# Two buffers for the odd units' features in an output stage, and its five queues in another order

## The chip, the core and the metric

The kernel runs on one core of one Trainium2 chip. The metric is the device time of one execution in microseconds (us). Three executions of the kernel before took 2344.98 to 2349.98 us, with a median of 2349.86 us. The engines are named as the profile names them: PE (TensorE, matmul), PEld (its weight loads), DVE (VectorE), ACT (ScalarE), POOL (GpSimd) and SP (SyncE, which here issues every DMA transfer, in program order).

## The reference: what is computed

The reference adds to x a gated linear attention. With `xn = layernorm(x)`, x of 2048 rows and 1024 columns:

```python
q, k, v = split(xn @ wqkv)                      # 32 heads of 32
phi = lambda a: concat(softmax(a @ w_phi), softmax(-(a @ w_phi)))
num = phi(q) @ (phi(k)^T v)                     # per head, 64 features
den = phi(q) . sum(phi(k)) + 1e-6
s   = (num / den) @ wo                          # 1024 x 1024
g   = silu((sigmoid(xn @ w_gate) * (xn @ w_up)) @ w_down)
out = x + s * g
```

All arrays are float32. The change touches only the last stage, which makes `num / den`, multiplies it by `wo`, and forms `x + s * g`.

## The kernel before, in words

A float32 product is made of three matmuls on rounded halves (high times high, high times low, low times high; helper `mm3`, lines 151 to 153), so each operand is split into a high part (a cast on ACT) and a low part (a subtraction on DVE). The large products use seven products of half-size blocks in place of eight; their names are B11, T2, B21, T3, T1, T4, B22. Earlier stages make q, k, v, the features, the gate g (kept in the DRAM tensor `g_d`) and the split blocks of `wo` (kept in `wo_d`). The scaled features of q, already divided by the denominators and transposed, lie in the DRAM tensor `et_d`.

The output stage works on eight pairs of row tiles, 256 rows each (`NTP = 8`). Its loop runs seven times over a list of names called `PAIR`, and once over a list called `LAST` for the eighth pair. In one pass the seven products of pair t are multiplied while the numerators of pair t+1 are made:

- `gB110` to `gT43` are the products: seven blocks, four steps each, three matmuls per step, so 28 steps and 84 matmuls. `gB220-` to `gB223-` belong to the pair before (a `-` behind a name means the pair before, a `+` the next).
- `nm011`, `nm010` and so on are the numerators: `nm` with the half of the heads (0 or 1), the band (0 or 1) and the block. Each is four matmuls of 128x256 (line 1139), eight such steps a pair. `cp` and `ad` bring a result out of PSUM: a copy on ACT (line 1146) and an addition on DVE (line 1148).
- A unit is one half of the heads of one pair. Unit 2t is the even half of pair t, unit 2t+1 the odd half. Each unit has features of two kinds. Those of band 0 are loaded as one transfer of 512 KB into slot 47 and split by `hi` (ACT, line 1127) and `lo` (DVE, line 1129) into slots 44 and 45. Those of band 1 are loaded already split, as two transfers of 512 KB (function `e_load`, line 1121), into slots 20 and 21. The names are `e10` and `e00+` for the first kind, `e11` and `e01+` for the second.
- `s11`, `sA`, `sB`, `sC` are subtractions on POOL (line 1155) that make the left operands of the seven products, and `x...h`, `x...l` their splits (lines 1167 and 1169). T1 and T3 have slots 24 and 25 in even pairs and 39 and 40 in odd ones; B21 and B22 have 26 and 27, or 41 and 42.
- `c2`, `c3` copy a PSUM bank on ACT (line 1994); `v...` takes a result out; `m...` and `a...` multiply by g and add x on POOL (lines 2020 and 2021); `l...` loads a block of g and one of x (lines 1961 and 1962); `y...` stores a block of the output (line 2026).
- `w0` to `w3`, in the first pass alone, store the last four blocks of g from slots 0 to 3 and then load the four `wo` blocks of product B22 into these slots.

The order on each engine is that of the list: the context `in_order` ties every instruction of PE, DVE, ACT, POOL and SP to the one ahead of it on its engine. So an SP instruction that waits for a semaphore holds all later transfers, whatever they need.

Of the kernel before, what the change touches and what calls it, by code (L numbers as in the profile page):

```python
# [35 lines left out]
class Ring:  # L36
# [3 lines left out]
    def next(self):  # L40
        self.n += 1
        return self.items[(self.n - 1) % len(self.items)]
# [5 lines left out]
B11, T2, T3, B21, T1, T4, B22 = range(7)  # L48
# [3 lines left out]
def hedgehog_glu_kernel(  # L52
# [41 lines left out]
    slots, blocks, where = {}, {}, {}  # L94
# [27 lines left out]
    def whole(i):  # L122
        return slots[i].rearrange("p a n -> p (a n)")
# [3 lines left out]
    def halves(*ids):  # L127
        found = [(slots[i][:, a], i) for i in ids for a in range(2)]
        half_of.update((id(o), (o, i)) for o, i in found)
        return [o for o, _ in found]  # L130
# [975 lines left out]
          T1: [], T4: [], B22: list(range(4))}  # L1106
    res = Ring(halves(49, 52))
    nmr, amm = Ring(banks[:4]), Ring(banks[4:])
    e_next = [0, 0]
    oraw = [slots[50], slots[51]]  # L1110

    def wo_prep(i, k):
# [1 line left out]

    nbank = {}

    def e_load(q):
        tp_, hb = divmod(e_next[q], 2)
        if tp_ < NTP:
            for part, o in ((1, slots[21]), (2, slots[20])) if q else ((0, slots[47]),):  # L1120
                nc.sync.dma_start(o.bitcast(F32).rearrange("p b n -> p (b n)").rearrange("p (c x) -> p c x", c=8),
                                  et_d[tp_].rearrange("p u a (s h x) -> p s h (u a) x", s=3, h=2)[:, part, hb])
        e_next[q] += 1

    def phi_part(part):
        if part == "hi":
            nc.scalar.copy(whole(44), whole(47))
        else:
            nc.vector.tensor_sub(whole(45), whole(47), whole(44).bitcast(F32))

    def numerators(hb, q, b):

        ph = [whole((44, 20)[q] + a).rearrange("p (c k t) -> p c k t", k=4, t=32) for a in range(2)]
        kg = slots[KVB[hb]][:, q].rearrange("p (k m) -> p k m", m=P)
        nbank[hb, q, b] = ps = nmr.next()
        for j in range(2):
            k = 2 * j + b
            for a in range(2):
                nc.tensor.matmul(ps[:, j * 256:(j + 1) * 256], kg[:, k], ph[a][:, :, k], start=a == 0, stop=a == 1)  # L1139
# [15 lines left out]
        nc.gpsimd.tensor_sub(o, a, b)  # L1155

    def o_slot(tp_, i):
        a, b = ((24, 26), (39, 41))[tp_ % 2]
        return {B11: 46, T2: 22, T4: 23, T1: a, T3: a + 1, B21: b, B22: b + 1}[i]

    def o_part(tp_, name, part):
        i, n, b = {"B11": (B11, 1, oraw[0][:, 0]), "T2": (T2, 1, o_new[:, 1]), "T4": (T4, 1, o_new[:, 0]),
                   "T13": (T1, 2, oraw[0]), "B2": (B21, 2, oraw[1])}[name]
        o = run(o_slot(tp_, i), n)
        hi, lo = [o[:, :, a] if n > 1 else o[:, 0, a] for a in range(2)]
        if part == "h":
            nc.scalar.copy(hi, b)
        else:
            nc.vector.tensor_sub(lo, b, hi.bitcast(F32))

    def attend():

        def o_operand(i):
            for part in "hl":
                o_part(0, i, part)

        def numerator(hb, q):
            for b in range(2):
                numerators(hb, q, b)
                for part in ("cp", "ad"):  # L1180
                    numerators_out(part, hb, q, b)
            if (hb, q) == (0, 1):
                o_operand("B11")
                o_sum("s11")
            if (hb, q) == (1, 1):
                for f, a in ((o_sum, "sB"), (o_operand, "B2"), (o_operand, "T2"), (o_sum, "sA"), (o_sum, "sC"),
                             (o_operand, "T13"), (o_operand, "T4")):
                    f(a)

        out = []  # L1190
        for hb in range(2):
            out += [(int,)] * 4 + [(phi_part, "hi"), (phi_part, "lo"), (e_load, 0)]
            for q in range(2):
                out += [(numerator, hb, q)] + [(e_load, 1)] * q
        return out
# [4 lines left out]
    first = [halves(i) for i in (50, 51, 54, 38)]  # L1200
# [190 lines left out]
    @contextmanager  # L1391
    def in_order(*engines):

        traced = nc.cur_bb.bb.instructions
        last = traced[-1]
        yield
        begin = next(k for k in reversed(range(len(traced))) if traced[k] is last) + 1
        for i in traced[begin:]:
            if i.engine in engines:
                if i.engine in queued:  # L1400
                    tc.add_manual_dep(i, queued[i.engine].name,
                                      mybir.DependencyInfo(mybir.DependencyClass.NoSync, mybir.DependencyReason.DATA),
                                      reason="in_order")
                queued[i.engine] = i
# [481 lines left out]
    for n in range(TT):  # L1886
        t = (light if (n + 1) * QA // TT > n * QA // TT else heavy).popleft()
        for hb in range(2):
            q_late(2 + (2 * n + hb) * 24 // 5, t, hb)
    for n, (i, j, cs) in enumerate(dsteps):  # L1890
# [3 lines left out]
        for c in cs:  # L1894
            for u in range(4):
                p = 4 * c + u
# [8 lines left out]
        k, odd = divmod(n - (ND - 2 * NJ) - 9, 3)  # L1905
# [20 lines left out]
        if n == ND - NJ:  # L1926
            assert not plan and len(retired) == 2
            for b in (2, 5, 6):
                block(f"x{b}", 4 * b, 4, F32R)
            block("fb", 44, 3, F32R)  # L1930
            sig_r.items = [slots[53][:, 0]] + halves(38)
            step(1000)
            for q in range(2):
                e_load(q)
            side.extend([lambda fn=fn, a=a: fn(*a) for fn, *a in attend()])
# [21 lines left out]
    def gx_load(n):  # L1957
        if n < len(result) and result[n] not in gxs:
            t, cols = rows(*result[n])
            g, xt = gxs[result[n]] = halves(47) if n == len(result) - 1 else [gx[(2 * n + a) % 6] for a in range(2)]  # L1960
            nc.sync.dma_start(g, g_d[t, :, cols])
            nc.sync.dma_start(xt, x[t * P:(t + 1) * P, cols])

    for n in range(2):
# [4 lines left out]


    PAIR = """
        gB110 xT13h- xT13l- sC- gB111 hi0 lo0 e10 gB112 nm011 cp011 ad011 aT4- lT1- yT4- gB113 c2
        gB220- nm010 e11 cp010 gB221- xT4h- xT4l- ad010 gB222- gB223-
        gT20 vB22- mB22- w0 w1 gT21 nm001 aB22- lT4 yB22- cp001 ad001 gT22 gT23 c3
        gB210 nm000 w2 w3 cp000 ad000 gB211 hi1 lo1 e00+ gB212 vT2 xB11h xB11l s11 gB213
        gT30 vB21 aB21 lB22 yB21 gT31 nm111 cp111 ad111 gT32 nm110 e01+ cp110 ad110 gT33 vT3
        gT10 nm101 cp101 ad101 gT11 gT12 nm100 cp100 ad100 gT13
        gT40 vT1 sB xB2h xB2l gT41 sA xT2h xT2l gT42 mT1 aT1 lB21 yT1 gT43 vT4""".split()

    LAST = ("gB110 xT13h- xT13l- sC- aT4- lT1- yT4- gB111 gB112 gB113 c2 gB220- gB221- xT4h- xT4l- gB222- gB223- "  # L1980
            "gT20 vB22- mB22- gT21 aB22- lT4 yB22- gT22 gT23 c3 vT2 gB210 gB211 rest gB212 gB213 gT30 vB21 aB21 yB21 "
            "gT31 gT32 gT33 vT3 gT10 gT11 gT12 gT13 gT40 vT1 mT1 aT1 yT1 gT41 gT42 gT43 vT4 aT4 gB220 gB221 gB222 yT4 end").split()
    abank, ys = {}, {}

    def products(tp_, i, k):
        if k == 0 and i in (B11, T1):
            abank[tp_, i] = amm.next()
        o = [h.rearrange("p (k t) -> p k t", t=P) for h in pair(o_slot(tp_, i))]
        ps = abank[tp_, {B21: B11, T4: T3, B22: T1}.get(i, i)]
        mm3(ps, (o[0][:, k], o[1][:, k]), pair(WO[i][k]), i in (B11, T1) and k == 0, k == 3, skip_group_check=True)  # L1990
# [57 lines left out]
    def last_weights(k):  # L2048
# [7 lines left out]
    i_ = lambda n: operand_of[n]  # L2056
    pair_forms = (
        (r"nm(\d)(\d)(\d)", True, lambda p, h, q, b: numerators(int(h), int(q), int(b))),
        (r"(cp|ad)(\d)(\d)(\d)", True, lambda p, part, h, q, b: numerators_out(part, int(h), int(q), int(b))),
        (r"(s11|sA|sB|sC)", True, lambda p, n: o_sum(n)),  # L2060
# [12 lines left out]
    def take(tp_, names):  # L2073
        for name in names:
            off = {"-": -1, "+": 1}.get(name[-1], 0)
            if 0 <= tp_ + off < (NTP if names is LAST else NTP - 1):
                f, found = next((f, m) for form, _, f in pair_forms for m in [re.fullmatch(form, name.rstrip("+-"))] if m)
                f(tp_ + off, *found.groups())

    queued.clear()  # L2080
    with in_order(*[getattr(mybir.EngineType, e) for e in ("PE", "DVE", "Activation", "Pool", "SP")]):
        for tp_ in range(NTP - 1):
            take(tp_, PAIR)
        gx_load(len(result) - 1)
        take(NTP - 1, LAST)

# [29 lines left out]
```

## Time and profile before

| what | value |
|---|---|
| three runs | 2344.98, 2349.98, 2349.86 us |
| the profiled execution's own time | 2348.69 us |
| its span in the trace | 2346.8 us |
| PE busy over the span | 2308.6 us (98%) |
| POOL, ACT, DVE busy | 1213.7, 1229.0, 1660.2 us |
| mean granted TensorE clock | 0.991 |
| last waits of the stages before the output stage | until 2118.41 us |
| first numerator step of pass 0 | 2121.96 us |

Times in views of the trace count from the start of the span. In rows of the timeline the columns are start, duration, engine, line, operation, tiles and count; in brackets stand the idle time before it and what ended that. A row of the windows view gives a stretch, its length, the busy time of PE, PEld, DVE, ACT and POOL with instruction counts, the granted clock, the busy share of the DMA engines and GB/s. In rows on SP the duration is that of the issue, not of the transfer.

### The profile page before, as it was taken

How to read it: one execution, taken by the hardware profiler on the slowest of the kernel's cores; microseconds unless marked ns; L12 is line 12 of the kernel's file. 1: busy time of each engine (PE TensorE's matmuls, PEld its weight loads, DVE VectorE, ACT ScalarE, POOL GpSimd, SP SyncE). 2: the span in 40 equal slices, each digit the busy share in tenths (PEclk: the TensorE clock that was granted, in tenths of full speed). 3: DMA queues.
4: the chain of work that ended last, by engine and by line, in shares of the span. 5: the costliest groups of instructions: out<-in, count | busy, mean ns of one | idle time of the engine just before them, and what ended most of it. 6: DMA issues, size and time to landing. Idle time of an engine off the chain costs nothing.

```text
span 2346.8 us, 31513 instructions
## 1 busy us (share of the span) xinstructions
PE 2308.6 (98%) x10533; PEld 1920.5 (82%) x10533; DVE 1660.2 (71%) x1906; ACT 1229.0 (52%) x1907; POOL 1213.7 (52%) x934
## 2 busy tenths in 40 slices
PE   9999999999999999999999999999999999998888
PEld 8888888888888888888888888888888888886777
DVE  7625777886788775778874656556899888865665
ACT  7345577776555555555555455543454345454443
POOL 1324436772241055665653766755787557624555
PEclk9999999999999999999999999999999999998989
DMA  8789977988878777887886877769888778998774
GB/s 298 262 307 356 345 289 281 351 312 307 282 270 283 270 248 274 303 310 265 271 321 212 290 237 245 240 219 350 268 255 284 232 230 267 299 327 285 231 217 152
DMA packets 340530, 648.05 MB, mean 276 GB/s; under 512 B 36752, under 2 KB 86160, under 8 KB 335760
## 3 DMA queue, kind: packets, MB, share of 16 engines
q1 hardware_dynamic: 340368, 646.05, 80.3%
q8 instruction: 82, 1.34, 0.2%
q14 instruction: 80, 0.66, 0.1%
HBM read 386.73 MB, written 259.19 MB: 275 GB/s over the span
## 4 chain that ended last, share of the span: by engine, by line
PE 90%; DMA 4%; POOL 2%; DVE 2%; issue 1%; ACT 1%; SPq 0%; POOLq 0%; ACTq 0%; DVEq 0%
PE bank L151 29%; PE bank L153 29%; PE bank L152 29%; DMA x<-et_d 2%; PE bank L749 1%; POOL fc L1155 1%; PE bank L386 1%; PE bank L1139 1%; DMA fc<-et_d 0%; POOL fc L2020 0%; PE bank L254 0%; DMA fa<-wv 0%; POOL fb L2021 0%; DMA fa<-w_gu 0%; DVE fc L733 0%
## 5 line engine op out<-in xcount | busy, mean ns | idle before, releaser
L152 PE MATMUL bank<-x,w 128*128 128x512 f32 x2248 | 874.9, 389 | 0.0
L151 PE MATMUL bank<-x,w 128*128 128x512 f32 x2248 | 872.8, 390 | 1.4 <-ACT fc L1456 0.6
L153 PE MATMUL bank<-x,w 128*128 128x512 f32 x2248 | 873.1, 389 | 0.0
L143 DVE TENSOR_TENSOR w<-fa,w 128x512 fp32r<-128x512 f32 (+2 forms) x344 | 392.5, 1144 | 287.8 <-ACT w L142 276.5
L151 PEld LDWEIGHTS bank<-x,w 128*128 128x128 f32 x2248 | 422.0, 188 | 90.0 <-ACT fc L1456 1.9
L153 PEld LDWEIGHTS bank<-x,w 128*128 128x128 f32 x2248 | 421.9, 188 | 87.9
L152 PEld LDWEIGHTS bank<-x,w 128*128 128x128 f32 x2248 | 422.0, 188 | 87.2 <-DVE x L143 0.4
L142 ACT CAST w<-fa 128x512 fp32r<-128x512 f32 (+2 forms) x344 | 273.0, 796 | 328.6 <-PE bank L152 129.0
L151 PE MATMUL bank<-w,x 128*128 128x512 f32 x704 | 275.9, 392 | 0.0
L152 PE MATMUL bank<-w,x 128*128 128x512 f32 x704 | 274.6, 390 | 0.2 <-DVE w L1321 0.2
L153 PE MATMUL bank<-w,x 128*128 128x512 f32 x704 | 274.7, 390 | 0.0
L153 PEld LDWEIGHTS bank<-w,x 128*128 128x128 f32 x704 | 132.3, 188 | 28.2 <-DVE x L1311 0.7
L152 PEld LDWEIGHTS bank<-w,x 128*128 128x128 f32 x704 | 132.5, 188 | 27.0 <-DVE w L1321 0.6
L151 PEld LDWEIGHTS bank<-w,x 128*128 128x128 f32 x704 | 132.5, 188 | 26.3
L143 DVE TENSOR_TENSOR x<-fb,x 128x512 fp32r<-128x512 f32 (+1 forms) x121 | 126.6, 1049 | 24.6 <-ACT x L142 23.9
L143 DVE TENSOR_TENSOR w<-fb,w 128x512 fp32r<-128x512 f32 (+2 forms) x82 | 81.9, 1001 | 46.1 <-ACT w L142 43.6
L1155 POOL TENSOR_TENSOR fc<-fc 128x512 f32<-128x512 f32 x32 | 55.5, 1744 | 105.2 <-DVE fc L1148 68.2
L142 ACT CAST x<-fb 128x512 fp32r<-128x512 f32 (+1 forms) x121 | 86.3, 715 | 21.6 <-DMA fb<-xr_d 7.1
L1148 DVE TENSOR_TENSOR fc<-fc,bank 64x512 f32<-64x512 f32 x64 | 43.9, 686 | 65.3 <-ACT fc L1146 64.5
L143 DVE TENSOR_TENSOR p<-fc,p 128x512 fp32r<-128x512 f32 (+1 forms) x68 | 55.1, 820 | 45.8 <-ACT p L142 41.8
L1456 ACT COPY fc<-bank 128x512 f32<-128x512 f32 x116 | 66.5, 583 | 38.2 <-PE bank L153 16.2
L142 ACT CAST w<-fb 128x512 fp32r<-128x512 f32 (+2 forms) x82 | 50.2, 612 | 60.0 <-PE bank L152 38.8
(403 smaller groups left out, 3782.4 us busy)
## 6 DMA issues: line engine op xcount, KB each, us to landing
m_d<-fc SPq DMA_DIRECT2D x168, 256.0 KB, 4.6
fa<-h_d SPq DMA_DIRECT2D x82, 512.0 KB, 5.4
fa<-wf_d SPq DMA_DIRECT2D x32, 1024.0 KB, 7.2
x<-m_d SPq DMA_DIRECT2D x128, 256.0 KB, 4.7
fa<-w_gu SPq DMA_DIRECT2D x102, 256.0 KB, 5.2
h_d<-fc SPq DMA_DIRECT2D x102, 256.0 KB, 4.9
et_d<-x SPq DMA_DIRECT2D x64, 384.0 KB, 6.0
fc<-qkv_d SPq DMA_DIRECT2D x86, 256.0 KB, 5.2
```

The costliest lines, as they stand in the source:

```text
L142: nc.scalar.copy(o[0], src)
L143: i = nc.vector.tensor_sub(o[1], src, o[0].bitcast(F32))
L151: nc.tensor.matmul(o, a[0], b[0], start=first, stop=False, **kw)
L152: nc.tensor.matmul(o, a[0], b[1], start=False, stop=False, **kw)
L153: last_mm[:] = [nc.tensor.matmul(o, a[1], b[0], start=False, stop=last, **kw).ins]
L386: nc.tensor.matmul(ps[:, gs], r[:, gs], bd[:, 4 * f + g], start=g == 0, stop=g == 3, skip_group_check=True)
L749: nc.tensor.matmul(kvb[g // 2][:, g % 2 * 256:g % 2 * 256 + 256], v[:, g].rearrange("p a f -> p (a f)"), ph[:, g].rearrange("p a f -> p (a ...
L1139: nc.tensor.matmul(ps[:, j * 256:(j + 1) * 256], kg[:, k], ph[a][:, :, k], start=a == 0, stop=a == 1)
L1148: nc.vector.tensor_add(o, o, y)
L1155: nc.gpsimd.tensor_sub(o, a, b)
L1456: nc.scalar.copy(o, banks[b])
```

## The change

Band 1 of the odd units, from unit 3 on, goes to slots 39 and 40 in place of 20 and 21, so that even and odd units no longer share a buffer. For that T1 and T3 use slots 24 and 25 in all pairs. Unit 3 is loaded ahead of the loop. The names in `PAIR` and `LAST` stand in another order; `e11` becomes `e11+` and `hi0` becomes `hi0+`, so these are issued one pass earlier.

```diff
+    def feature_slots(unit):
+        return 39 if unit > 1 and unit % 2 else 20
...
-            for part, o in ((1, slots[21]), (2, slots[20])) if q else ((0, slots[47]),):
+            a = feature_slots(e_next[1])
+            for part, o in ((1, slots[a + 1]), (2, slots[a])) if q else ((0, slots[47]),):
...
-        ph = [whole((44, 20)[q] + a).rearrange("p (c k t) -> p c k t", k=4, t=32) for a in range(2)]
+        first = feature_slots(steps_of[1] // 2) if q else 44
+        steps_of[q] += 1
+        ph = [whole(first + a).rearrange("p (c k t) -> p c k t", k=4, t=32) for a in range(2)]
...
-        a, b = ((24, 26), (39, 41))[tp_ % 2]
-        return {B11: 46, T2: 22, T4: 23, T1: a, T3: a + 1, B21: b, B22: b + 1}[i]
+        b = (26, 41)[tp_ % 2]
+        return {B11: 46, T2: 22, T4: 23, T1: 24, T3: 25, B21: b, B22: b + 1}[i]
...
     PAIR = """
-        gB110 xT13h- xT13l- sC- gB111 hi0 lo0 e10 gB112 nm011 cp011 ad011 aT4- lT1- yT4- gB113 c2
-        gB220- nm010 e11 cp010 gB221- xT4h- xT4l- ad010 gB222- gB223-
-        gT20 vB22- mB22- w0 w1 gT21 nm001 aB22- lT4 yB22- cp001 ad001 gT22 gT23 c3
-        gB210 nm000 w2 w3 cp000 ad000 gB211 hi1 lo1 e00+ gB212 vT2 xB11h xB11l s11 gB213
-        gT30 vB21 aB21 lB22 yB21 gT31 nm111 cp111 ad111 gT32 nm110 e01+ cp110 ad110 gT33 vT3
-        gT10 nm101 cp101 ad101 gT11 gT12 nm100 cp100 ad100 gT13
-        gT40 vT1 sB xB2h xB2l gT41 sA xT2h xT2l gT42 mT1 aT1 lB21 yT1 gT43 vT4""".split()
+        gB110 xT13h- xT13l- gB111 lo0 e10 gB112 nm011 gB113 c2 cp011 ad011
+        gB220- nm010 cp010 ad010 aT4- lT1- yT4- gB221- gB222- gB223-
+        gT20 vB22- mB22- gT21 aB22- lT4 yB22- e01+ sC- gT22 nm001 gT23 c3 cp001 ad001
+        gB210 nm000 cp000 ad000 gB211 hi1 lo1 e00+ xT4h- xT4l- gB212 vT2 xB11h xB11l s11 gB213
+        gT30 vB21 aB21 lB22 yB21 w0 w1 gT31 nm111 cp111 ad111 gT32 nm110 e11+ cp110 ad110 gT33 vT3
+        gT10 w2 w3 gT11 nm101 cp101 ad101 gT12 nm100 cp100 ad100 gT13
+        gT40 vT1 sB xB2h xB2l gT41 sA xT2h xT2l hi0+ gT42 mT1 aT1 lB21 yT1 gT43 vT4""".split()
...
     with in_order(*[getattr(mybir.EngineType, e) for e in ("PE", "DVE", "Activation", "Pool", "SP")]):
+        phi_part("hi")
+        e_load(1)
         for tp_ in range(NTP - 1):
             take(tp_, PAIR)
```

In `LAST` the names `aT4- lT1- yT4-`, `sC-` and `xT4h- xT4l-` move later in the same way.

The first place is SP in a middle pass of the loop, from the store of T4 (`out<-fb`) on. `x_4` and `fa` are the two feature buffers of band 1 (slots 20 and 21, 39 and 40), `fc<-et_d` is the band 0 load, `g_d` and `x` are the loads of the gate and of x. Before:

```order
L2026 DMA out<-fb_0_99 128x512
L1121 DMA x_4_15714<-et_d 128x8x128 x2
L1961 DMA fc_101<-g_d 128x512
L1962 DMA fc_101<-x 128x512
L2026 DMA out<-fc_101 128x512
L1121 DMA fc_101<-et_d 128x8x128
L1961 DMA p_3_16019<-g_d 128x512
L1962 DMA p_3_16019<-x 128x512
L2026 DMA out<-fc_101 128x512
L1121 DMA x_4_15714<-et_d 128x8x128 x2
```

Now:

```order
L2032 DMA out<-fb_0_99 128x512
L1967 DMA fc_101<-g_d 128x512
L1968 DMA fc_101<-x 128x512
L2032 DMA out<-fc_101 128x512
L1125 DMA x_4_15714<-et_d 128x8x128 x2
L1125 DMA fc_101<-et_d 128x8x128
L1967 DMA p_3_16019<-g_d 128x512
L1968 DMA p_3_16019<-x 128x512
L2032 DMA out<-fc_101 128x512
L1125 DMA fa_16018<-et_d 128x8x128 x2
```

The first pair of band 1 rows of before is the odd unit of this pass (`e11`); now the first is the even unit of the next pass (`e01+`), and the second is the odd unit of the next pass (`e11+`) in its own buffer.

The second place is PE at the numerator steps of the odd half (`nm111` and `nm110`), around T3's products (`bank_108`):

```order
 L153 MATMUL bank_108<-x_6_15598,x_7_15715 128x512
-L1139 MATMUL bank_102<-x_4_15714,p_9711 128x256 x4
+L1145 MATMUL bank_102<-fa_16018,p_9711 128x256 x4
 L151 MATMUL bank_108<-x_6_15598,x_7_15715 128x512
 L152 MATMUL bank_108<-x_6_15598,x_7_15715 128x512
 L153 MATMUL bank_108<-x_6_15598,x_7_15715 128x512
-L1139 MATMUL bank_103<-x_4_15714,p_9711 128x256 x4
+L1145 MATMUL bank_103<-fa_16018,p_9711 128x256 x4
```

The steps stand where they stood, and read the new buffer.

The third place is SP in the first pass. `g_d<-x_5` are the last four stores of the gate, `x_6<-wo_d` the four loads of `wo` for B22. Before:

```order
L1121 DMA x_4_15714<-et_d 128x8x128 x2
L1961 DMA fc_101<-g_d 128x512
L1851 DMA g_d<-x_5_11982 128x512 x4
L1113 DMA x_6_16061<-wo_d 128x1024 x2
L1961 DMA p_3_16019<-g_d 128x512
L1962 DMA p_3_16019<-x 128x512
L1113 DMA x_6_16061<-wo_d 128x1024 x2
L1121 DMA fc_101<-et_d 128x8x128
L1961 DMA fc_101<-g_d 128x512
L1962 DMA fc_101<-x 128x512
L2026 DMA out<-fc_101 128x512
L1121 DMA x_4_15714<-et_d 128x8x128 x2
```

Now:

```order
L1125 DMA x_4_15714<-et_d 128x8x128 x2
L1125 DMA fc_101<-et_d 128x8x128
L1967 DMA fc_101<-g_d 128x512
L1968 DMA fc_101<-x 128x512
L2032 DMA out<-fc_101 128x512
L1857 DMA g_d<-x_5_11982 128x512 x4
L1113 DMA x_6_16114<-wo_d 128x1024 x2
L1125 DMA fa_16018<-et_d 128x8x128 x2
L1113 DMA x_6_16114<-wo_d 128x1024 x2
```

The stores and the four `wo` loads moved behind the store of B21 (`out<-fc`), and the band 1 load of the next pass (the last row of before, `e01+`) moved from behind them to ahead of them.

More of the change, by code (lines that the diff above doesn't have):

```diff
@@ L1108, in hedgehog_glu_kernel @@
     nmr, amm = Ring(banks[:4]), Ring(banks[4:])
-    e_next = [0, 0]
+    e_next, steps_of = [0, 0], [0, 0]
     oraw = [slots[50], slots[51]]
@@ L1971, in hedgehog_glu_kernel @@
     PAIR = """
-        gB110 xT13h- xT13l- sC- gB111 hi0 lo0 e10 gB112 nm011 cp011 ad011 aT4- lT1- yT4- gB113 c2
-        gB220- nm010 e11 cp010 gB221- xT4h- xT4l- ad010 gB222- gB223-
-        gT20 vB22- mB22- w0 w1 gT21 nm001 aB22- lT4 yB22- cp001 ad001 gT22 gT23 c3
-        gB210 nm000 w2 w3 cp000 ad000 gB211 hi1 lo1 e00+ gB212 vT2 xB11h xB11l s11 gB213
-        gT30 vB21 aB21 lB22 yB21 gT31 nm111 cp111 ad111 gT32 nm110 e01+ cp110 ad110 gT33 vT3
-        gT10 nm101 cp101 ad101 gT11 gT12 nm100 cp100 ad100 gT13
-        gT40 vT1 sB xB2h xB2l gT41 sA xT2h xT2l gT42 mT1 aT1 lB21 yT1 gT43 vT4""".split()
-    LAST = ("gB110 xT13h- xT13l- sC- aT4- lT1- yT4- gB111 gB112 gB113 c2 gB220- gB221- xT4h- xT4l- gB222- gB223- "
-            "gT20 vB22- mB22- gT21 aB22- lT4 yB22- gT22 gT23 c3 vT2 gB210 gB211 rest gB212 gB213 gT30 vB21 aB21 yB21 "
+        gB110 xT13h- xT13l- gB111 lo0 e10 gB112 nm011 gB113 c2 cp011 ad011
[5 more added lines that the diff above has]
+        gT40 vT1 sB xB2h xB2l gT41 sA xT2h xT2l hi0+ gT42 mT1 aT1 lB21 yT1 gT43 vT4""".split()
+    LAST = ("gB110 xT13h- xT13l- gB111 gB112 gB113 c2 aT4- lT1- yT4- gB220- gB221- gB222- gB223- "
+            "gT20 vB22- mB22- gT21 aB22- lT4 yB22- sC- gT22 gT23 c3 vT2 gB210 xT4h- xT4l- gB211 rest gB212 gB213 gT30 vB21 aB21 yB21 "
             "gT31 gT32 gT33 vT3 gT10 gT11 gT12 gT13 gT40 vT1 mT1 aT1 yT1 gT41 gT42 gT43 vT4 aT4 gB220 gB221 gB222 yT4 end").split()
```

## The prediction

> **What bounds the kernel now.** I read the page first (the span and its slices), then the waits of PE, then the windows of the output stage, and last the timeline around one wait.
>
> ```profile
> span 2346.8 us, 31513 instructions
> PE   9999999999999999999999999999999999998888
> PEclk9999999999999999999999999999999999998989
> ```
>
> PE is full for 36 slices and falls to eight tenths in the last four, which are the output stage; the granted clock dips in the same slices. Only there is time to be had. The waits of PE from 2085 us to the end name the cause:
>
> ```profile
> PE bank L1139 <- DMA x<-et_d: 26.6, 6, 7.9
> ```
>
> The six waits, each with its idle time in brackets, and the stretches between them:
>
> ```profile
> 2151.02 1.19 PE L1139 MATMUL bank<-x,p 128*128 128x256 f32 x4 [7.88 <-DMA x<-et_d]
> 2192.86 0.72 PE L1139 MATMUL bank<-x,p 128*128 128x256 f32 x4 [2.84 <-DMA x<-et_d]
> 2221.89 0.98 PE L1139 MATMUL bank<-x,p 128*128 128x256 f32 x3 [4.12 <-DMA x<-et_d]
> 2250.86 0.77 PE L1139 MATMUL bank<-x,p 128*128 128x256 f32 x2 [4.30 <-DMA x<-et_d]
> 2280.14 0.77 PE L1139 MATMUL bank<-x,p 128*128 128x256 f32 x2 [3.81 <-DMA x<-et_d]
> 2309.93 0.81 PE L1139 MATMUL bank<-x,p 128*128 128x256 f32 x3 [3.67 <-DMA x<-et_d]
> ```
>
> ```profile
> 2123.33:2142.98 19.65, 19.46 (x98) 16.16 (x96) 11.39 (x14) 9.92 (x17) 7.17 (x6) 1.00 0.80 266
> 2142.98:2192.86 49.88, 38.48 (x179) 31.89 (x178) 28.04 (x32) 20.48 (x31) 28.03 (x18) 0.90 0.79 242
> 2192.86:2221.89 29.03, 24.91 (x116) 20.74 (x117) 17.80 (x19) 12.75 (x19) 15.95 (x10) 0.93 0.72 222
> 2221.89:2250.86 28.97, 24.67 (x117) 20.65 (x117) 17.80 (x19) 12.75 (x19) 15.96 (x10) 0.91 0.72 218
> 2250.86:2280.14 29.28, 25.47 (x116) 21.29 (x117) 17.80 (x19) 12.74 (x19) 15.97 (x10) 0.91 0.69 211
> 2280.14:2309.93 29.79, 26.12 (x116) 21.79 (x117) 17.80 (x19) 12.74 (x19) 15.96 (x10) 0.90 0.69 212
> 2309.93:2346.80 36.87, 32.40 (x145) 27.07 (x145) 14.75 (x19) 8.50 (x13) 18.86 (x14) 0.92 0.40 137
> ```
>
> The first wait stands at nm011 of the second pass (the even unit), the other five at nm111 of the passes after it (the odd unit). Why the odd unit is late shows in the queue ahead of its two loads:
>
> ```profile
> 2208.92 2.27 POOL L1155 TENSOR_TENSOR fc<-fc 128x512 f32<-128x512 f32 x1
> 2211.15 1.29 POOL L2021 TENSOR_TENSOR fb<-fb,fc 128x512 f32<-128x512 f32 x1
> 2212.85 0.42 SPq L2026 DMA_DIRECT2D out<-fb  x1
> 2213.37 1.78 SPq L1121 DMA_DIRECT2D x<-et_d  x2
> ```
>
> POOL does sC, then aT4; the store of T4 waits for that until 2212.44, and the feature loads stand behind the store in SP's order. They go out at 2213.37, and PE gets them at 2221.89, 8.5 us later. They could not go out long before either: both units share slots 20 and 21, so nm010 must have read the even unit first.
>
> **The price of one wait** is more than the idle time, since PE runs slower behind it. Behind the 1.89 us wait that opens the stage:
>
> ```profile
> 2118.41 0.50 PE L151 MATMUL bank<-x,fb 128*128 128x512 f32 x1 [1.89 <-DVE x L1878]
> 2120.26 0.63 PE L153 MATMUL bank<-x,fb 128*128 128x512 f32 x1
> 2120.68 0.63 PE L151 MATMUL bank<-x,fb 128*128 128x512 f32 x1
> 2122.65 0.39 PE L151 MATMUL bank<-x,fb 128*128 128x512 f32 x1
> 2122.88 0.39 PE L152 MATMUL bank<-x,fb 128*128 128x512 f32 x1
> ```
>
> Matmuls start 0.42 us apart at 2120 and 0.23 apart at 2122.65, so a product step of three costs 0.69 us at full clock. The undisturbed stretch 2123.33 to 2142.98 (clock 1.00) holds 23 such steps, 15.9 us, and seven numerator steps, which leaves 0.54 us for each of these. A whole pair has five steps and one numerator step more: 19.65 + 3.45 + 0.54 = 23.6 us. The four middle pairs take 29.03, 28.97, 29.28 and 29.79; take off each one's wait, and PE is still busy for 24.91, 24.67, 25.47 and 26.12, that is 1.1 to 2.5 us over 23.6: the slow clock.
>
> The Trainium skill ("TensorE: Matmul & The Clock Gate", part 1 on the HAM clock gate) has the clock fall to half after an idle window of about 3.4 us, and come back after a like time of work. The halving and the length of the slow spell agree with these rows; that a wait of 1.89 us is enough does not, and the measurement decides. By that rule, small waits that remain would cost only themselves.
>
> **What the change takes away.** Edit by edit.
>
> - *Own buffer for odd units, loads a pass ahead.* `e11+` goes out behind nm110 and the store of B21 of the pass before, and is wanted at the next nm111, nearly a whole pair later (some 17 us). `e01+` goes out behind the store of B22, some 15 us ahead of its old place. Both landed within 9.7 us at worst:
>
> ```profile
> DMA to landing us min/median/max: 4.3/6.4/9.7
> ```
>
>   So I take all six waits as gone. The four middle pairs give 117.07 - 4 x 23.6 = 22.7 us. The wait at 2192.86 gives its 2.84. Behind 2309.93 there are 42 product steps and four numerator steps, 29.0 + 2.2 = 31.2 us, against 32.40 busy: 1.2. Together 26.7 us for the five odd waits. The first wait gives 7.88 and its slow spell: the stretch to 2192.86 holds 43 product and 12 numerator steps, 29.7 + 6.5 = 36.2 us, against 38.48 busy: 2.3; together 10.2. The sum is 36.9 us.
>
> - *T1 and T3 in one buffer.* The split `xT13` of a pass stands behind gB110 and the last read of the old operands, gT13, four product steps (2.8 us) ahead of it. Nothing waits: cost 0, at most some 0.5 us if ACT ran that far ahead.
>
> - *sC and xT4 later.* sC now comes behind aB22 on POOL, about 6.6 us behind gB223; the T4 operand is wanted at gT40, some 13 us behind gB223. POOL is busy for 16 us of a pair, so it keeps up at 23.6. Cost 0; without that cover, xT4 is late by what POOL is late.
>
> - *w0 to w3 later, in the first pass only.* Here is a new wait.
>
> ```profile
> 2133.66 1.30 POOL L2021 TENSOR_TENSOR fc<-fc 128x512 f32<-128x512 f32 x1
> 2126.68 2.70 SPq L1851 DMA_DIRECT2D g_d<-x  x4
> 2133.89 0.80 SPq L1113 DMA_DIRECT2D x<-wo_d  x2
> 2140.58 3.30 SPq L1121 DMA_DIRECT2D x<-et_d  x2
> x<-wo_d SPq DMA_DIRECT2D x16, 512.0 KB, 7.1
> ```
>
>   Before, the four stores of g go out from 2126.68 and the first `wo` load 7.2 us later, since it overwrites what they read. Now they stand behind aB21, which ends at 2134.96, and its store: from about 2135.4. The first `wo` load then goes out at about 2142.6, the fourth, behind the two `e11+` loads, at about 2145.6, and lands 7.1 us later at 2152.7. Products reach gB223 of the second pass, free of the old wait, at 2142.98 + 0.54 + 0.69 (nm011, gB113) + 3 x 0.69 + 0.54 = 2146.8. So PE waits 5.9 us in gB220 to gB223, and the slow spell adds 2.3: 8.2 us. Bounds: 0 if stores and loads land much faster on a quieter queue, 10.2 if all lands as late as 2155. I take 8.2, the value of the median landing. What is queued behind these loads on SP (lB21, yT1, `e10`) is not wanted before vB21 and hi1, which this wait delays as well.
>
> - *hi0 a pass earlier, unit 3 ahead of the loop.* 1 MB more ahead of eight `wo` loads that are wanted 20 us later, and one cast of 1.05 us at a place where ACT is half idle (12.7 of 29 us busy). Cost 0.
>
> The sum: 2348.69 - 36.9 + 8.2 = 2320.0. The median of the runs shown is 1.2 us above the profiled execution, so 2321 us, 1.2% less.
>
> **What is the limit next.** The band 0 features still have one slot, and their load `e10` stands in SP behind the store of T1. This closes a loop:
>
> ```profile
> 2199.37 0.64 PE L1139 MATMUL bank<-fb,p 128*128 128x256 f32 x4
> 2200.04 0.58 ACT L1146 COPY fc<-bank 64x512 f32<-64x512 f32 x1 [1.26 <-PE bank L1139]
> 2201.49 3.53 POOL L1155 TENSOR_TENSOR fc<-fc 128x512 f32<-128x512 f32 x2 [8.85 <-DVE fc L1148]
> 2206.80 2.16 POOL L2021 TENSOR_TENSOR fc<-fc 128x512 f32<-128x512 f32 x1
> 2210.07 0.52 SPq L1121 DMA_DIRECT2D fc<-et_d  x1
> 2216.09 1.05 ACT L1127 CAST fb<-fc 128x1024 fp32r<-128x1024 f32 x1 [1.15 <-DMA fc<-et_d]
> 2217.18 1.23 DVE L1129 TENSOR_TENSOR fb<-fc,fb 128x1024 fp32r<-128x1024 f32 x1 [1.45 <-ACT fb L1127]
> ```
>
> From nm100 over cp, ad, sB, sA, mT1, aT1, yT1, `e10`, its landing (6.0 us from issue to hi1) and lo1 it takes 2218.41 - 2199.37 = 19.0 us; nm101 and one step follow, 1.2 us, and nm100 stands again: 20.3 us. That is under 23.6, with 3.3 us to spare. Before, the waits of 4 us hid it.
>
> **Rivals.**
>
> *The band 0 loop or the DMA engines take part of it back.* A pair keeps the DMA engines busy for 0.71 of 29 us, 20.6 us; in 23.6 us that is 0.87, so landings may lengthen. The spare 3.3 us are gone when `e10` takes 9.3 us, near the longest landing seen. At 10 us each pass waits 0.7 us at nm101 and pays some 1.7 us of slow clock: six times 2.4 is 14, and the time 2335. For it: hi1 already waited 1.15 us for this load. Against: its landing sits in a gap of the queue, behind transfers of only 0.75 MB. With the skill's rule the clock would stay up, and the time be 2321 + 6 x 0.7 = 2325.
>
> *The `wo` loads are not late.* Then 8.2 us more is gained: 2313. For it: stores of 256 KB from a quiet queue. Against: the 7.2 us above.
>
> *No change.* The wait moves to another operand by as much as it was (`xT4` behind a late POOL, say, since sC, s11 and sB now follow each other closely): pairs of 29 us, 2347. POOL's 16 us speak against it.
>
> *Slower.* The same loop, with landings above 13.3 us: then a pair is 20.3 - 6.0 + 13.3 + 1.7 = 29.3 us, as now. At 15 us it is 31, five pairs lose 8.5 us, less the 2 won in the second pass: 2356. It needs a queue that stays full while loads run a pass ahead; a share of 0.87 speaks against it.
>
> **Chances.** Forecast 0.62 (its own range 2315 to 2329), loop in part 0.20, no late `wo` loads 0.08, no change 0.05, slower 0.05. About 0.2%, or 4.7 us, is what a measurement can tell here. Faster is 0.62 + 0.20 + 0.08 = 0.90, same 0.05, slower 0.05. The range runs from all waits gone with no new one (2312, and 1 us of spread) to somewhat beyond the second case: 2311 to 2339.
>
> **What would show it.** Right: no wait of L1139 for `x<-et_d` or `fa<-et_d`; pairs of 23.6 to 24.5 us with the clock at 1.00; one wait of 4 to 8 us on a DMA of `wo_d` near 2145; DMA share near 0.87. Wrong: waits at nm101 for lo1 (L1129 in before), a clock below 0.95 in the middle pairs, PE waits on xT4's split, or SP held behind `e01+` so that g or x come late for vB21.

## The result and the profile after

The changed kernel takes 2312.78 us (median, 2311.92 to 2313.67); the kernel before, beside it, 2347.42 us (2343.85 to 2349.98). The ratio is 0.9854, with a 95% interval of 0.9836 to 0.9871: 1.5% faster. The forecast was 2321 us, 1.2% less. The time lies 2.2 us below the forecast's own range (2315 to 2329) and near the low end of the wide one (2311 to 2339).

The page of the changed kernel, its span and PE's slices:

```profile
span 2311.7 us, 31526 instructions
PE   9999999999999999999999999999999999999899
PEclk9999999999999999999999999999999999999999
```

The fall over the last four slices is gone, but for one slice, and so is the dip of the clock. All that PE waits for from 2085 us to the end:

```profile
PE bank L151 <- DMA x<-wo_d: 5.9, 2, 5.7
PE bank L151 <- DVE x L1884: 1.7, 1, 1.7
PE bank L151 <- DVE x L1175: 1.3, 1, 1.3
PE bank L151 <- ACT bank L2000: 0.2, 1, 0.2
```

No wait for `et_d` is left. The windows of the changed kernel, one pass of the loop each, from nm111 to nm111, and the rest (columns as before: length, busy PE, PEld, DVE, ACT, POOL, granted clock, DMA share, GB/s):

```profile
2160.78:2183.92 23.14, 23.14 (x118) 19.59 (x116) 16.18 (x19) 11.67 (x18) 16.00 (x10) 1.00 0.74 227
2183.92:2207.05 23.13, 23.13 (x117) 19.58 (x116) 17.28 (x20) 12.74 (x20) 16.02 (x10) 1.00 0.91 270
2207.05:2230.18 23.13, 23.13 (x117) 19.58 (x116) 17.12 (x20) 12.61 (x19) 16.00 (x10) 1.00 0.92 275
2230.18:2253.32 23.14, 23.14 (x118) 19.58 (x116) 16.91 (x19) 12.19 (x19) 16.01 (x10) 1.00 0.89 270
2253.32:2276.45 23.13, 23.13 (x117) 19.58 (x116) 17.52 (x20) 13.25 (x21) 16.02 (x10) 1.00 0.90 274
2276.45:2311.70 35.25, 30.78 (x146) 25.66 (x144) 17.12 (x23) 9.86 (x16) 21.93 (x15) 1.00 0.45 150
```

Each pass takes 23.13 us and PE is busy for all of it; before it took 29.0 to 29.8. From the second of these passes on the DMA engines work at 0.89 to 0.92 of their time.

The wait that the change adds stands in the second pass (timeline of PE, and SP's four `wo` loads):

```profile
2136.57 0.79 SPq L1113 DMA_DIRECT2D x<-wo_d  x2
2137.46 1.24 SPq L1125 DMA_DIRECT2D fa<-et_d  x2
2138.74 5.16 SPq L1113 DMA_DIRECT2D x<-wo_d  x2
2140.04 0.47 PE L151 MATMUL bank<-x,x 128*128 128x512 f32 x1 [1.25 <-DVE x L1175]
2141.64 0.50 PE L151 MATMUL bank<-x,x 128*128 128x512 f32 x1 [0.19 <-DMA x<-wo_d]
2148.32 0.79 PE L151 MATMUL bank<-x,x 128*128 128x512 f32 x1 [5.73 <-DMA x<-wo_d]
2149.34 0.63 PE L153 MATMUL bank<-x,x 128*128 128x512 f32 x1
2154.78 0.39 PE L153 MATMUL bank<-x,x 128*128 128x512 f32 x1
```

PE waits 5.73 us and runs at half clock until 2154.5: the 15 matmuls from 2148.32 to 2155.01, where nm001 starts, take 6.7 us in place of 3.4 (15 times 0.23), so 3.3 us more.

Where the 35.1 us between the two spans come from: the first product of the loop (gB110) starts at 2118.41 before and at 2114.43 after, and from there it takes 228.4 and 197.3 us. So 31.1 us are the output stage. The other 4.0 were there well before: SP issues the same load of `w_down` at 2069.92 before and at 2065.94 after, and the first load that the change adds, that of unit 3, goes out only at 2103.13. The experiment on the kernel before, below, bears on them.

### The profile page after: what moved, and what is told of

Read it like the earlier page. It is cut to its first block, busy times and chain, and to the rows that moved or that the text cites. A ratio compares the mean times of both kernels' runs of the same rounds, so it can differ in the third digit from the quotient of the medians.

```text
span 2311.7 us, 31526 instructions
## 1 busy us (share of the span) xinstructions
PE 2294.9 (99%) x10533; PEld 1911.0 (83%) x10533; DVE 1664.3 (72%) x1906; ACT 1231.0 (53%) x1907; POOL 1219.2 (53%) x934
## 5 line engine op out<-in xcount | busy, mean ns | idle before, releaser
L143 DVE TENSOR_TENSOR w<-fa,w 128x512 fp32r<-128x512 f32 (+2 forms) x344 | 397.5, 1159 | 294.3 <-ACT w L142 273.5
L151 PE MATMUL bank<-w,x 128*128 128x512 f32 x720 | 282.0, 392 | 0.0
L153 PE MATMUL bank<-w,x 128*128 128x512 f32 x720 | 280.9, 390 | 0.0
L152 PE MATMUL bank<-w,x 128*128 128x512 f32 x720 | 280.6, 390 | 0.0
L153 PEld LDWEIGHTS bank<-w,x 128*128 128x128 f32 x720 | 135.2, 188 | 29.2 <-DVE x L1317 1.0
L152 PEld LDWEIGHTS bank<-w,x 128*128 128x128 f32 x720 | 135.3, 188 | 26.9 <-DVE w L1327 0.3
L151 PEld LDWEIGHTS bank<-w,x 128*128 128x128 f32 x720 | 135.2, 188 | 26.6
L1161 POOL TENSOR_TENSOR fc<-fc 128x512 f32<-128x512 f32 x32 | 49.8, 1566 | 78.0 <-DVE fc L1154 33.3
```

The costliest lines, as they stand in the source:

```text
L143: i = nc.vector.tensor_sub(o[1], src, o[0].bitcast(F32))
L151: nc.tensor.matmul(o, a[0], b[0], start=first, stop=False, **kw)
L152: nc.tensor.matmul(o, a[0], b[1], start=False, stop=False, **kw)
L153: last_mm[:] = [nc.tensor.matmul(o, a[1], b[0], start=False, stop=last, **kw).ins]
```

## The experiments

**The `wo` loads of the first pass earlier.** Of the changed kernel, only the place of the last stores of g (`ws`) and of the loads for B22 is another:

```diff
-        ... lT4 yB22- e01+ sC- gT22 ...
+        ... lT4 yB22- e01+ ws sC- gT22 ...
-        ... hi1 lo1 e00+ xT4h- ...
+        ... hi1 lo1 e00+ w0 w1 w2 w3 xT4h- ...
-        gT30 vB21 aB21 lB22 yB21 w0 w1 gT31 ...
-        gT10 w2 w3 gT11 ...
+        gT30 vB21 aB21 lB22 yB21 gT31 ...
+        gT10 gT11 ...
```

> The changed kernel, but in the first pass the four stores of g go out behind the first e01+ loads, and the four wo loads of B22 behind e00+, about 6 us earlier than in the changed kernel (where the first goes out at 2136.57 and the wait for the third or fourth ends at 2148.32). Theory: the 5.9 us of PE waits on wo_d in the second pass are the price of moving w0 to w3 behind the store of B21, and nothing else waits there; without them PE also keeps its full clock behind (12 matmuls at 0.43 us apart now, 2.7 us lost). Expected: no PE wait on wo_d, 2304 to 2306 us. Rival: the DMA engines are simply full in the first pass, so the loads land as late whenever they go out, or e01+ and lB22 come late instead: 2311 to 2315, with a wait of like size on another load.

Measured: 2304.3 us (2303.07 to 2305.73), ratio to the kernel before 0.9826 (0.981 to 0.9843). SP and all of PE's waits from 2085 us on:

```profile
2133.58 1.74 SPq L1113 DMA_DIRECT2D x<-wo_d  x4
```

```profile
PE bank L151 <- DVE x L1884: 1.8, 1, 1.8
PE bank L151 <- ACT bank L2000: 0.2, 1, 0.2
```

Counted from gB110 (2115.64 here, 2114.43 in the changed kernel) the first of these loads goes out after 17.9 us in place of 22.1, the last by 19.7 in place of 29.5, and no wait on `wo_d` or anything behind it is left. The theory holds: late `wo` loads were the price of the change. The medians put it at 8.5 and 9.0 us (against the two measurements of the changed kernel, 2312.78 and, below, 2313.25), the ratios to the kernel before at 6.6 and 8.2; the prediction had 8.2. This version is the fastest of all that ran.

It also shows what the 1.25 us wait ahead of gB220 in the changed kernel is. The profile names a split on DVE (`DVE x L1175`); here gB220 (second row) starts without a wait while that split still runs:

```profile
2139.47 1.67 DVE L1175 TENSOR_TENSOR x<-fc,x 128x1024 fp32r<-128x1024 f32 x1
2139.84 0.40 PE L151 MATMUL bank<-x,x 128*128 128x512 f32 x1
```

So gB220 does not need the split, and its wait belongs to the `wo` loads as well.

**One buffer, new order.** The changed kernel with slots 20 and 21 for all units:

```diff
-        return 39 if unit > 1 and unit % 2 else 20
+        return 20
-        gB220- nm010 cp010 ad010 aT4- lT1- yT4- ...
+        gB220- nm010 e11 cp010 ad010 aT4- lT1- yT4- ...
-        ... lT4 yB22- e01+ sC- ...     ... nm110 e11+ cp110 ...
+        ... lT4 yB22- sC- ...          ... nm110 e01+ cp110 ...
-        e_load(1)
```

> The changed kernel with one band 1 buffer (slots 20 and 21 for every unit), so the loads cannot go a pass ahead: e11 goes out at once behind nm010, ahead of the loads of g and x and the store of T4; e01+ behind nm110. All else in the new order. Theory that the second buffer is needed: from nm010 to nm111 PE has 13 product and 2 numerator steps, 9.9 us, and from nm110 to nm011 12 and 2, 9.3 us, against 7 to 9 us from issue to landing plus up to 1.4 us of issue, so most passes wait 0 to 2 us in one or both places with a slow spell behind: 2322 to 2332. Rival, that the place in the queue was all of it: at most 1 us per pass, 2313 to 2319. Either way the first pass shows e01+ late by some 8 us at nm011 of the second pass, which hides the wait on wo_d.

Measured: 2323.56 us (2322.02 to 2324.25), ratio 0.9907 (0.9892 to 0.9922). PE's waits at the numerator steps (line 1145):

```profile
PE bank L1145 <- DMA x<-et_d: 13.2, 8, 7.4
PE bank L1145 <- DVE fb L2013: 1.5, 2, 0.8
PE bank L1145 <- DVE fb L1175: 1.0, 1, 1.0
```

The order alone brings two thirds of the gain (22 us, where the changed kernel gained 35 in its first measurement and 32 in its second): the load is no longer behind the store of T4, and the waits of 3 to 4 us shrink to 0.4 to 1.9. But they come at both ends of the pass, since each load can only start when the other unit has been read. The theory that the second buffer is needed for the rest holds, at the low end of what was expected. Part of this is the first pass, where 7.4 us of `e01+` replace the wait on `wo_d`.

**Two buffers, old order.** A first version kept `e11+` at the old place of `e11`:

```diff
-        gB220- nm010 e11 cp010 ...
+        gB220- nm010 e11+ cp010 ...
```

> The kernel before in its old order, with only the second band 1 buffer (odd units from unit 3 on in slots 39 and 40, T1 and T3 in 24 and 25), e11 replaced by e11+ at its old place behind the store of T4, and unit 3 loaded ahead of the loop. Theory that the buffer is what counts: the five waits at nm111 go, the first one (7.88 us, e01+ behind the wo loads) stays and replaces the 5.9 us wait on wo_d: pairs of 23.1 to 23.5 us and 2313 to 2319 us. Rival, that the order counts: with hi0 and e01+ at their old places PE waits in each pass for even features or for lo1, pairs of 25 us or more, 2325 to 2335.

Measured: 2314.27 us (2311.55 to 2317.93). This kernel leaves a part out: loads are counted in the order of the units, `e11+` stood ahead of the `e01+` that it must follow, and so no band 1 features are loaded behind unit 4; the later passes multiply old ones. It says nothing on the order. It gives a floor, though: with 1 MB to 2 MB of loads missing from each pass, the only wait for features is the first one (5.7 us at nm011 of the second pass), and its passes from then on take 23.12 to 23.13 us. Those of the changed kernel, with all loads, take 23.13, so the loads cost it nothing there. The mended version:

```diff
-        gB220- nm010 e11 cp010 ...
+        gB220- nm010 cp010 ...
-        ... gT32 nm110 e01+ cp110 ...
+        ... gT32 nm110 e01+ e11+ cp110 ...
```

> The kernel before in its old order with only the second band 1 buffer: odd units from unit 3 on in slots 39 and 40, T1 and T3 in 24 and 25, unit 3 loaded ahead of the loop, and the load of the odd unit moved from behind nm010 to directly behind e01+ (behind nm110), for the next pass. This mends the earlier kernel of the old order. Theory that the buffer is what counts for the five odd waits, and that hi0, sC, xT4 and w0 to w3 were moved for nothing in the steady passes: only the first wait, nm011 of the second pass on e01+, stays with 5.5 to 8.6 us and its slow spell; pairs of 23.1 to 23.5 us; 2312 to 2318. Rival, that the new order is needed too: with 2 MB of features behind one another, e01+ lands too late for nm011 (9.3 us behind nm110) or lB21 too late for vB21, 0.5 to 2 us in each pass, with slow spells 2320 to 2330.

Measured: 2320.28 us (2318.62 to 2321.76), ratio 0.9893 (0.9875 to 0.9911). This is in the rival's range and not in the 2312 to 2318 that I expected. PE's waits for features, with nm110 (`fa,p`) and the `e01+` loads of one pass:

```profile
2146.02 1.20 PE L1145 MATMUL bank<-x,p 128*128 128x256 f32 x4 [7.61 <-DMA x<-et_d]
2172.86 0.71 PE L1145 MATMUL bank<-x,p 128*128 128x256 f32 x4 [1.13 <-DMA x<-et_d]
2186.36 0.64 PE L1145 MATMUL bank<-fa,p 128*128 128x256 f32 x4
2188.90 1.51 SPq L1125 DMA_DIRECT2D x<-et_d  x2
2196.84 0.72 PE L1145 MATMUL bank<-x,p 128*128 128x256 f32 x4 [0.64 <-DMA x<-et_d]
2220.75 0.71 PE L1145 MATMUL bank<-x,p 128*128 128x256 f32 x4 [0.57 <-DMA x<-et_d]
2245.05 0.73 PE L1145 MATMUL bank<-x,p 128*128 128x256 f32 x4 [0.97 <-DMA x<-et_d]
2269.24 0.73 PE L1145 MATMUL bank<-x,p 128*128 128x256 f32 x4 [0.83 <-DMA x<-et_d]
```

The five waits at nm111 are gone with the buffer alone. The first wait stays, and a new small one comes: passes no longer slowed let PE reach nm011 0.6 to 1.1 us ahead of `e01+`, which leaves 2.5 us behind nm110, held up in the queue, and is there 7.9 us after that. Both theories had a part: the buffer alone (25 us, where the changed kernel run beside it gained 32) ends the odd waits, and the earlier `e01+` is worth about 1 us a pass as well. The passes take 23.9 to 24.3 us.

The changed kernel itself, run beside this one:

> The changed kernel itself beside the two runs with the old order and the early wo loads, for a direct comparison: 2311 to 2315, with the 5.7 us wait on wo_d again (4 to 7 us).

Measured: 2313.25 us (2311.13 to 2315.12), ratio 0.9861 (0.9845 to 0.9876), with these waits for `wo_d` in the second pass:

```profile
2140.05 0.48 PE L151 MATMUL bank<-x,x 128*128 128x512 f32 x1 [0.80 <-DMA x<-wo_d]
2141.96 0.50 PE L151 MATMUL bank<-x,x 128*128 128x512 f32 x1 [0.49 <-DMA x<-wo_d]
2147.29 0.80 PE L151 MATMUL bank<-x,x 128*128 128x512 f32 x1 [4.36 <-DMA x<-wo_d]
```

**The kernel before once more.**

> The kernel before once more, for what its runs differ by. The changed kernel reached gB110 of the first pass 4.0 us earlier (2114.43 against 2118.41) though its instructions up to there are the same on PE, ACT, DVE and POOL. Theory that this is spread between executions of the earlier stages: this one reaches gB110 anywhere from 2113 to 2119, and takes 228 us from there to its end. Rival, that the change moves it: again within 1 us of 2118.4.

Measured: 2344.54 us, span 2342.7. The first product of the loop:

```profile
2115.49 0.50 PE L151 MATMUL bank<-x,fb 128*128 128x512 f32 x1 [1.55 <-DVE x L1878]
```

It starts at 2115.49 here and at 2118.41 in the other execution, and the stage takes 227.2 us against 228.4. So the start of the stage moves by 3 us between executions of one kernel; over all kernels here, alike up to there but for the load of unit 3, it lies between 2113.97 and 2118.41. I put the 4.0 us between the first two profiles down to this spread. The stage itself repeats within 1.2 us before; in the two executions of the changed kernel it took 197.3 and 194.3. Of these 3.0 us, 1.5 are shorter waits in the second pass (5.65 us in place of 7.17), and 1.5 a shorter slow spell behind them (1.7 in place of 3.2).

**The band 0 load later**, to measure what time is spare on the loop that the prediction named as the next limit. In the first kernel `e10` goes behind the store of T4, in the second behind that of B22:

```diff
-        gB110 xT13h- xT13l- gB111 lo0 e10 gB112 ...
+        gB110 xT13h- xT13l- gB111 lo0 gB112 ...
-        ... aT4- lT1- yT4- gB221- ...
+        ... aT4- lT1- yT4- e10 gB221- ...            (first)
-        ... lT4 yB22- e01+ sC- ...
+        ... lT4 yB22- e10 e01+ sC- ...               (second)
```

> The changed kernel with the band 0 load e10 behind the store of T4 in place of ahead of the load lT1: it goes out about 2.6 us later in each pass. In the changed kernel lo1 ends at 2184.61 and nm101 starts at 2187.65, so 3.0 us are spare. Theory that e10's loop is the next limit, with about 3 us to spare: no wait, or a few tenths at nm101; 2312 to 2316. Rival, that landings lengthen in a full queue and the spare time is already used in most passes: waits of 1 us or more at nm101, 2318 to 2330.

> The changed kernel with e10 behind the store of B22, about 5.6 us later in each pass. Theory: the loop is over its spare 3.0 us by 2.6 us; PE waits about 2 to 3 us at nm101 in passes 1 to 6, and pays 1 to 2.5 us of slow clock behind each: pairs of 26 to 28 us, 2327 to 2342. Rival, that e10 is not on any path that matters (hi1 could come later still, or the passes run ahead): under 1 us per pass, 2312 to 2317.

Measured: 2320.57 us (2318.49 to 2321.37), ratio 0.9892 (0.9878 to 0.9907), and 2336.74 us (2334.97 to 2343.18), ratio 0.9968 (0.9956 to 0.998). First one pass of the changed kernel: nm001, `e10`, hi1, lo1 and nm101.

```profile
2199.57 0.53 SPq L1125 DMA_DIRECT2D fc<-et_d  x1
2201.26 0.64 PE L1145 MATMUL bank<-fb,p 128*128 128x256 f32 x4
2205.43 1.05 ACT L1131 CAST fb<-fc 128x1024 fp32r<-128x1024 f32 x1 [1.02 <-DMA fc<-et_d]
2206.52 1.23 DVE L1133 TENSOR_TENSOR fb<-fc,fb 128x1024 fp32r<-128x1024 f32 x1 [1.28 <-ACT fb L1131]
2210.78 0.64 PE L1145 MATMUL bank<-fb,p 128*128 128x256 f32 x4
```

Then the like of the first experiment, where PE waits for hi1 and then for lo1:

```profile
2200.99 0.64 PE L1145 MATMUL bank<-fb,p 128*128 128x256 f32 x4
2202.62 0.53 SPq L1125 DMA_DIRECT2D fc<-et_d  x1
2209.86 1.05 ACT L1131 CAST fb<-fc 128x1024 fp32r<-128x1024 f32 x1 [5.71 <-DMA fc<-et_d]
2210.97 0.39 PE L1145 MATMUL bank<-fb,p 128*128 128x256 f32 x1 [0.29 <-ACT fb L1131]
2212.23 0.64 PE L1145 MATMUL bank<-fb,p 128*128 128x256 f32 x3 [0.88 <-DVE fb L1133]
```

In the changed kernel lo1 ends at 2207.75 and nm101 starts at 2210.78: 3.0 us spare. The first experiment missed what I expected (2312 to 2316): `e10` goes out 3.3 us later as measured from nm001, not 2.6, and in this pass it takes 7.2 us from the issue to hi1 in place of 5.9. That makes 4.7 us, 1.7 over the spare time, and the passes from 2210 us on take 23.7 to 24.9 us in place of 23.13. So the loop is the next limit, with 3.0 us to spare where 3.3 were forecast. The landing is not fixed: over the last four passes it took 5.9 to 7.2 us here and 5.9 to 6.6 in the changed kernel. Whether its new place in the queue lengthens it, these few passes don't show. The second experiment came out as the theory had it: waits in five passes, and behind those of 2.6 us or more a slow spell. The two kinds of wait at nm101, and three of its rows:

```profile
PE bank L1145 <- ACT fb L1131: 9.6, 5, 3.1
PE bank L1145 <- DVE fb L1133: 4.0, 5, 0.9
2193.12 0.39 PE L1145 MATMUL bank<-fb,p 128*128 128x256 f32 x1 [2.62 <-ACT fb L1131]
2221.34 0.39 PE L1145 MATMUL bank<-fb,p 128*128 128x256 f32 x1 [0.95 <-ACT fb L1131]
2249.04 0.58 PE L1145 MATMUL bank<-fb,p 128*128 128x256 f32 x1 [3.15 <-ACT fb L1131]
```

Its passes take 27 to 28 us, from nm101 to nm101. The waits alternate between long and short. `e10` goes out 20.3 us behind the nm101 of the pass before, whether that pass had a slow spell or not; a slow spell makes PE come later to the next nm101, and so it waits less there.

## Why the prediction was right, and where it was off

- *The cause of the waits*, shown. The odd units' loads stood behind the store of T4 and shared a buffer. Either cure alone ends the waits of 3 to 4 us (one buffer in the new order 2323.6 us, two buffers in the old order 2320.3), and only both end all waits for features (2312.8). The prediction took them as one edit and did not say that each brings two thirds or three quarters of the gain by itself.
- *The size of the five odd waits*, 26.7 us. The pair was put at 23.6 us and is 23.13. The step that failed is the price of the clean pair. The product step of 0.69 us holds, but a numerator step costs 0.48 (nm011 at 2116.61, the next product at 2117.09) and not 0.54: I took it as what was left of a stretch of the first pass in which PE also waits 0.2 us for ACT (L1994). Eight such steps make the 0.5 us. Over the five passes from 2160.78 to 2276.45 that is 118.0 against 115.7, 2.3 us.
- *The first wait and the `wo` loads.* The mechanism came as forecast, the size only roughly. Forecast: 5.9 us of waits and 2.3 of slow clock, 8.2 in all. Measured: 5.9 us for `wo_d`, 1.25 ahead of gB220 and 3.3 of slow clock, 10.4 in all; in the second execution 7.4. The first load goes out at 2136.57 (2142.6 forecast) and the wait is over at 2148.32 (2152.7 forecast); less the 4.0 us by which the stage starts earlier, these are 2.0 and 0.4 us off. That the end fits so well is luck in part: the first load left 2.0 us sooner than forecast, but the issue of the last two took 5.16 us. The 1.25 us I had not forecast; the profile puts them down to a split of DVE, the run with the earlier loads to the `wo` loads. The upper bound of 10.2 us is a slip: with 2155 as the end it is 8.2 + 2.3 = 10.5.
- *Edits at no cost* (T1 and T3 in one buffer, sC, xT4 and hi0 moved, unit 3 ahead): no wait of PE on any of them. They weren't tried one by one; with hi0, sC and xT4 at their old places (two buffers, old order) nothing waits for them either, so that the runs show no use of moving them. There PE waits 0.6 to 1.1 us in each pass for `e01+`, though, which may hide a smaller wait.
- *The sum.* The stage became 31.1 us shorter against 28.7 forecast (36.9 less 8.2). Gains that the forecast lacked: 2.3 us are the pair; 0.4 the stretch from the last nm111 to the end (35.25 us against 36.87 less 1.2); 0.7 a wait of PE for DVE (0.67 us at 2177.53 before) that is gone; and 1.6 a slow spell behind the opening wait, which I had left in: before, from gB110 at 2118.41 to full clock at 2122.65; after, from 2114.43 on, no spell at all. This last one is luck, since the spell comes in some executions and not in others (last section). The larger slow clock (1.0) and the 1.25 us take 2.3 back. That makes 2.7 us, within 0.3 of the 2.4. The remaining 4.0 us by which the profile undercut the forecast I put down to the spread of earlier stages; without them the profiled execution would have taken 2317.6 us. So 2312.78 is not the rival without late `wo` loads, though its number, 2313, is the same.
- *Rivals.* The band 0 loop takes nothing back at 3.0 us spare, but a load that goes out 3.3 us later already does. The DMA share of 0.87 became 0.89 to 0.92, and from issue to hi1 `e10` takes 5.9 to 6.6 us in the last five passes, where it took 5.7 to 6.5.
- *The Trainium skill's rule on the clock gate.* That small waits cost only themselves holds here up to 1.25 us. It does not hold for waits of 2.6 to 3.3 us, which all brought a slow spell though they are shorter than the rule's idle window: see the last section.

## What to carry to other kernels

Read a late load from both sides: what its queue holds ahead of it, and which read must free its buffer; the two can be worth the same, and each hides the other. When a wait goes, list what else was due behind it: here four weight loads that could go late only as long as PE stood still, 8 to 9 us that a better place in the queue gave back. And take the clean length of a pass from a stretch without any disturbance, or say how far off it may be.

## What the runs showed of the hardware

Behind a short wait the half clock comes in one execution and not in another. At nearly the same length of the wait that opens the stage, PE ran slow behind it or did not. Two rows of the kernel before, then two of the changed kernel, where the matmuls of the next step are 0.39 us long (full clock) and not 0.63:

```profile
2118.41 0.50 PE L151 MATMUL bank<-x,fb 128*128 128x512 f32 x1 [1.89 <-DVE x L1878]
2120.26 0.63 PE L153 MATMUL bank<-x,fb 128*128 128x512 f32 x1
```

```profile
2114.43 0.50 PE L151 MATMUL bank<-x,fb 128*128 128x512 f32 x1 [1.75 <-DVE x L1884]
2115.24 0.39 PE L151 MATMUL bank<-x,fb 128*128 128x512 f32 x1
```

Over the output stages of all ten profiles here: waits up to 1.25 us, like those in the old order with two buffers, never brought a slow spell; those from 1.5 to 1.9 us brought one in some executions (1.85, 1.88 and 1.89 us) and none in others (1.55, 1.60, 1.75, 1.81, 1.86, 1.87 and 1.89); those of 2.6 us or more always did. The Trainium skill ("TensorE: Matmul & The Clock Gate", part 1) has a window of about 3.4 us that runs freely, and a change to full clock that depends on where in it the first matmul falls. The same for the fall to half would fit these rows, but no run here shows the window itself. The Trainium skill's idle time of a whole window was not needed here: 1.85 us were enough. A slow spell cost 1.1 to 3.3 us.
